# Seven block products for one more group, and the inverse deviation from ScalarE, in a fused attention and MLP kernel

## The chip, the cores and the metric

The kernel runs on one core of a Trainium2 chip. The metric is device time in microseconds (us) of one execution; less is better. Each kernel was run several times beside the kernel before on the same chip. A ratio below is the mean time of one kernel's fast runs over that of the other's fast runs of the same rounds, so it is not quite the ratio of the medians that are quoted beside it. A run counts as slow, and not as fast, when it is over 1.5% above the fastest of the same kernel; the ratios leave these out.

## The reference

Sliding-window attention for 8 batches, 8 heads, 576 positions and 64 channels per head, then a layer norm and a two-layer MLP (512 to 2048 to 512) with a residual:

```python
scores = scale * q @ k.T;  mask = (rel >= 0) & (rel < 64)
attn = softmax(where(mask, scores, -1e9));  x = attn @ v      # (8, 576, 512) after the heads are joined
mu = mean(x);  var = mean((x - mu) ** 2)
xn = (x - mu) / sqrt(var + 1e-06) * g_ln
out = x + relu(xn @ w_ch1) @ w_ch2
```

## The kernel before

The rows are worked in nine groups: groups 0 to 7 are the first 512 positions of each batch, group 8 the last 64 positions of all batches (the "tail", four blocks of 128 rows that are prepared during periods 3, 5 and 7). A *period* is the MLP of one group; the attention of the next group is spread over it in numbered *slots*, one behind each unit of matmuls. The order of every engine's queue is the order in which the program is written.

A block's way through the layer norm: `b_step` (attention times v, normalisation and statistics, on VectorE), `z_step` (the normalised rows `z`, in fp16), `zt_step` (`z` transposed into `zT`, which the first layer multiplies; by a DMA for groups 2 to 7 except the last block of groups 3 and 5, by TensorE for the rest). For groups 2 to 8 `z` is GpSimd's work:

```python
nc.gpsimd.tensor_scalar(out=ve, in0=var, scalar1=1.0, scalar2=EPS, op0=ALU.mult, op1=ALU.add)
nc.gpsimd.tensor_tensor(out=rs, in0=ve, in1=mhalf, op=ALU.pow)
nc.gpsimd.tensor_scalar(out=nm, in0=mu, scalar1=rs, scalar2=-1.0, op0=ALU.mult, op1=ALU.mult)
nc.gpsimd.tensor_scalar(out=z, in0=xv, scalar1=rs, scalar2=nm, op0=ALU.mult, op1=ALU.add)
```

For groups 0 and 1 VectorE only subtracts the mean; the factor (by Newton steps, `newton`) is applied to the output.

The second layer of groups 2 to 8 is done with seven block products instead of eight: 112 matmuls of 256 columns in place of 64 of 512. It needs sums of W2's blocks once (`w2_sums`, eight VectorE operations, two in period 1 and six in period 2) and sums of the hidden activations for every group (`s_sums`, VectorE), and VectorE adds each product to the output (`post`). Groups 0 and 1 use plain products.

```python
# period 1 (g == 1) prepares group 2, slots of b_step, z_step, zt_step
at((13, 17, 20, 23)[j], b_step, 2, j)
at((13, 17, 20, 23)[j], z_step, 2, j)
at((18, 21, 24, 27)[j], zt_step, 2, j)
# ... cut ...
# later periods prepare group b, and the tail's block i
at((2, 7, 12, 17)[j], b_step, b, j);  at((2, 7, 12, 17)[j], z_step, b, j)
ts = (10, 11, 14, 20) if n else (1, 2, 5, 11)
at(ts[2], b_step, NGRP - 1, i);  at(ts[2], z_step, NGRP - 1, i);  at(ts[3], zt_step, NGRP - 1, i)
```

The softmax here doesn't subtract the row's maximum and nothing guards it: scores larger than these inputs give would overflow.

## Time and profile before

| | before |
|---|---|
| median of 4 runs | 314.07 us |
| span of the profiled run | 313.0 us |
| TensorE (PE) busy | 298.9 us, 95% |
| VectorE (DVE), ScalarE (ACT), GpSimd (POOL) busy | 66%, 49%, 53% |
| granted TensorE clock | 0.999 |

The page's first part gives each engine's busy time with its share of the span and its number of instructions:

```profile
PE 298.9 (95%) x3041; PEld 194.1 (62%) x3041; DVE 205.2 (66%) x385; ACT 153.4 (49%) x258; POOL 166.3 (53%) x251
```

The table of windows gives busy time of each engine per stretch; its columns are the stretch, its length, and busy us with the number of instructions for PE, PEld (weight load), DVE, ACT and POOL, then the granted clock, the DMA share and GB/s:

```profile
75.00:98.00 23.00, 22.36 (x240) 11.98 (x238) 14.82 (x38) 9.02 (x15) 12.74 (x23) 1.00 0.62 137
160.00:190.00 30.00, 29.99 (x322) 19.74 (x320) 21.11 (x40) 16.07 (x27) 19.91 (x31) 1.00 1.02 228
```

TensorE has no gap to speak of. Anything that makes it wait is paid in full, and little can be gained elsewhere.

The groups of GpSimd instructions that make `z` (line, engine, operation, output and inputs, count, then busy us and mean ns of one, then idle time ahead of them):

```profile
L345 POOL TENSOR_SCALAR z<-xn,rsz 128x512 f16<-128x512 f32 x28 | 25.3, 902 | 2.9
L343 POOL TENSOR_TENSOR rsz<-rsz,mhalf 128x1 f32<-128x1 f32 x28 | 19.3, 689 | 2.3
L344 POOL TENSOR_SCALAR rsz<-mvg,rsz 128x1 f32<-128x1 f32 x28 | 13.4, 480 | 2.8
L342 POOL TENSOR_SCALAR rsz<-mvg 128x1 f32<-128x1 f32 x28 | 10.7, 382 | 60.4 <-DVE mvg L328 59.8
```

The issue queue of SyncE near the end of period 1, from the timeline (start, us, queue, line, operation):

```profile
93.08 0.33 SPq L430 DMA_DIRECT2D out_dram<-xn  x1
93.50 1.21 SPq L353 DMA_TRANSPOSE zT<-z  x1
```

The last `zT` transpose of group 2 stands behind a store there, and group 2's first matmul starts at 96.43 us: just in time.

### The profile page before, as it was taken

The numbers are of one execution on the slowest core, as the hardware profiler recorded it, in microseconds if no ns is written. First come the engines' busy times: TensorE is split into PE (matmuls) and PEld (weight loads), VectorE is DVE, ScalarE is ACT, GpSimd is POOL, SyncE is SP. The second block draws the span as 40 slices with busy tenths as digits, with TensorE's granted clock in tenths as the row PEclk, the third lists the DMA queues.
The fourth block names the chain that finished last, engine by engine and source line by source line (L and its number), as shares of the span: only waits on it lengthen the run. The fifth ranks groups of instructions, "written<-read, shape, count | busy, mean of one in ns | idle before, by whom it ended". The sixth has DMA issues, their size and how long they took to land.

```text
span 313.0 us, 7473 instructions
## 1 busy us (share of the span) xinstructions
PE 298.9 (95%) x3041; PEld 194.1 (62%) x3041; DVE 205.2 (66%) x385; ACT 153.4 (49%) x258; POOL 166.3 (53%) x251
## 2 busy tenths in 40 slices
PE   6988998899999999999999999999999999999992
PEld 4457544497554468646964686459646855784582
DVE  1689585855674996589666965896669636751642
ACT  1496633477416752776247526762475058306500
POOL 7578666454760798369814983698145506200000
PEclk9999999999999999999999999999999999999999
DMA  8999999998866996798179997993690393003013
GB/s 192 267 390 290 320 336 272 280 304 184 159 144 196 268 206 105 243 312 147 37 212 316 203 149 219 316 142 67 209 172 19 62 209 117 2 2 134 0 36 101
DMA packets 109892, 57.42 MB, mean 183 GB/s; under 512 B 79841, under 2 KB 100833, under 8 KB 109858
## 3 DMA queue, kind: packets, MB, share of 16 engines
q1 hardware_dynamic: 108944, 54.02, 69.1%
q0 software_dynamic: 768, 2.80, 3.7%
q8 instruction: 24, 0.39, 0.5%
q10 hardware_dynamic: 146, 0.13, 0.1%
q14 instruction: 10, 0.08, 0.1%
HBM read 38.80 MB, written 9.44 MB: 154 GB/s over the span
## 4 chain that ended last, share of the span: by engine, by line
PE 74%; DMA 10%; DVE 7%; SPq 4%; POOL 2%; ACT 1%; issue 1%; POOLq 0%; ACTq 0%
PE hps L392 30%; PE pA L464 11%; PE pC L464 7%; PE pB L464 7%; PE ch L404 6%; DMA w2s<-in_moe_w_ch_dram 4%; DMA qk<-in_k_dram 4%; PE xps L317 3%; PE sc L283 3%; PE hph L513 3%; PE tp L226 2%; SPq L141 2%; DVE sS L443 2%; DMA w1s<-in_moe_w_ch_dram 2%; SPq L89 1%; DVE pt L297 1%
## 5 line engine op out<-in xcount | busy, mean ns | idle before, releaser
L392 PE MATMUL hps<-zT,w1g 128*128 128x512 f16 x480 | 110.4, 379 | 0.0
L396 ACT ACTIVATE hrT<-hps 128x512 f16<-128x512 f32 x120 | 71.9, 599 | 50.7 <-PE hps L392 47.2
L392 PEld LDWEIGHTS <-w1g 128*128 128x128 f16 x480 | 44.6, 98 | 49.3 <-issue 1.0
L290 ACT ACTIVATE pt<-sc 128x512 f16<-128x512 f32 x72 | 39.0, 595 | 29.8 <-DVE xn L471 15.6
L464 PEld LDWEIGHTS <-sS 128*128 128x128 f16 x448 | 43.3, 98 | 5.1
L342 POOL TENSOR_SCALAR rsz<-mvg 128x1 f32<-128x1 f32 x28 | 10.7, 382 | 60.4 <-DVE mvg L328 59.8
L128 POOL CAST qk<-qk 128x1024 f16<-128x1024 f32 x32 | 35.1, 1112 | 13.4 <-DMA qk<-in_q_dram 6.9
L464 PEld LDWEIGHTS <-hrT 128*128 128x128 f16 x336 | 32.6, 98 | 5.2
L212 ACT COPY qkT<-tp 128x1024 f16<-128x1024 f16 x16 | 16.1, 1012 | 35.2 <-PE tp L226 26.1
L297 DVE TENSOR_TENSOR pt<-pt,mask 128x1024 f16<-128x1024 f16 x32 | 25.4, 800 | 11.9 <-ACT pt L290 11.9
L471 DVE TENSOR_TENSOR xn<-pA,xn 128x512 f32<-128x512 f32 x28 | 19.2, 686 | 21.1 <-PE pA L464 21.1
L443 DVE TENSOR_TENSOR sS<-hrT 128x512 f16<-128x512 f16 (+1 forms) x42 | 24.8, 591 | 10.2 <-ACT hrT L396 10.2
L464 PE MATMUL pA<-wT,sS 128*128 128x256 f16 x224 | 26.9, 273 | 0.0
L345 POOL TENSOR_SCALAR z<-xn,rsz 128x512 f16<-128x512 f32 x28 | 25.3, 902 | 2.9
L464 PE MATMUL pC<-w2s,sS 128*128 128x256 f16 x224 | 26.8, 273 | 0.0
L325 DVE BATCH_NORM_STATS2 stats<-xn 128x6 f32<-128x512 f32 x36 | 25.0, 695 | 1.2
L323 DVE TENSOR_TENSOR xn<-xps,rcp 128x512 f32<-128x512 f32 x36 | 24.9, 692 | 1.2
L513 PE MATMUL hph<-zT,w1g 128*128 128x256 f16 x192 | 23.2, 272 | 2.3 <-ACT zT L360 1.1
L320 DVE RECIPROCAL rcp<-xps 128x8 f32<-128x8 f32 x36 | 7.4, 205 | 26.8 <-PE xps L317 26.8
L404 PE MATMUL ch<-w2s,hrT 128*128 128x512 f16 x96 | 23.1, 380 | 0.0
L513 PEld LDWEIGHTS <-w1g 128*128 128x128 f16 x192 | 18.3, 98 | 5.1 <-issue 2.6
L317 PEld LDWEIGHTS <-pt 128*64 128x64 f16 x576 | 12.2, 110 | 14.4 <-issue 6.4
(85 smaller groups left out, 395.1 us busy)
## 6 DMA issues: line engine op xcount, KB each, us to landing
out_dram<-xn SPq DMA_DIRECT2D x34, 256.0 KB, 2.6
qk<-in_q_dram SPq DMA_DIRECT2D x16, 512.0 KB, 6.2
qk<-in_k_dram SPq DMA_DIRECT2D x16, 512.0 KB, 7.4
v<-in_v_dram SPq DMA_DIRECT2D x32, 256.0 KB, 6.5
w2s<-in_moe_w_ch_dram SPq DMA_DIRECT2D x12, 512.0 KB, 5.7
w1s<-in_moe_w_ch_dram SPq DMA_DIRECT2D x4, 512.0 KB, 6.7
tk<-in_k_dram SPq DMA_DIRECT2D x8, 256.0 KB, 4.7
tv<-in_v_dram SPq DMA_DIRECT2D x8, 256.0 KB, 5.3
```

Of the source, the lines that this page charges most:

```text
L128: nc.gpsimd.tensor_copy(out=dst[:, :].rearrange("p (a j) e d -> p a e j d", j=j), in_=t[:, :].rearrange("p (a e j d) -> p a e j d", e=2, j ...
L290: nc.scalar.activation(out=o, in_=i, func=AF.Exp, bias=0.0, scale=scale)
L297: nc.vector.tensor_tensor(out=ptv, in0=ptv, in1=mb, op=ALU.mult)
L323: nc.vector.tensor_tensor(out=xn, in0=xps[:, :, 0:D], in1=rcp_b, op=ALU.mult)
L325: nc.vector.bn_stats(out=stats, in_=xv)
L345: nc.gpsimd.tensor_scalar(out=z, in0=xv, scalar1=rs, scalar2=nm, op0=ALU.mult, op1=ALU.add)
L392: nc.tensor.matmul(out=hps, lhsT=w1g[:, kc, 128 * hc:128 * (hc + 1)], rhs=zT[g][:, kc, :], start=(kc == 0), stop=(kc == NKC - 1),)
L396: nc.scalar.activation(out=hrT[:, hc, :], in_=hps, func=AF.Relu, bias=0.0, scale=1.0)
L404: nc.tensor.matmul(out=ch[kb], lhsT=hrT[:, hc, 128 * kb:128 * (kb + 1)], rhs=w2s[:, hc, :], start=(hc == 0), stop=(hc == NHC - 1),)
L443: nc.vector.tensor_tensor(out=o, in0=x, in1=y, op=op)
L464: nc.tensor.matmul(out=bank[which][:, p, :], lhsT=a[:, c, 128 * p:128 * p + 128], rhs=wv[:, c, :], start=(first and p == 0 and c == 0), st ...
L513: nc.tensor.matmul(out=hps[:, e], lhsT=w1g[:, kc, 128 * hc:128 * (hc + 1)], rhs=zT[g][:, kc, 256 * half:256 * half + 256], start=(kc == 0) ...
```

## The change

Intent: save TensorE time by giving group 1 the seven products too, and unload GpSimd by computing the inverse deviation on ScalarE, as exp(-ln(var + eps)/2), with one table set that holds both functions. The core of the diff:

```diff
+    nc.scalar.preload_act_table_set("natural_log_exp_and_others")
 # z_step, groups 1 to 8 (group 0 keeps the subtraction alone)
-        nc.gpsimd.tensor_scalar(out=ve, in0=var, scalar1=1.0, scalar2=EPS, op0=ALU.mult, op1=ALU.add)
-        nc.gpsimd.tensor_tensor(out=rs, in0=ve, in1=mhalf, op=ALU.pow)
-        nc.gpsimd.tensor_scalar(out=nm, in0=mu, scalar1=rs, scalar2=-1.0, op0=ALU.mult, op1=ALU.mult)
-        nc.gpsimd.tensor_scalar(out=z, in0=xv, scalar1=rs, scalar2=nm, op0=ALU.mult, op1=ALU.add)
+        nc.scalar.activation(out=lv, in_=var, func=AF.Ln, bias=epst[:, 0:1], scale=1.0)
+        nc.scalar.activation(out=rs, in_=lv, func=AF.Exp, bias=0.0, scale=-0.5)
+        eng = nc.vector if g == 1 else nc.gpsimd
+        eng.tensor_scalar(out=z, in0=xv, scalar1=mu, scalar2=rs, op0=ALU.subtract, op1=ALU.mult)
 # seven products from group 1 on
-        units, s_sums = mlp_units(g, (8, 16)[g] if g < 2 else 0, g == 0, g > 1)
+        units, s_sums = mlp_units(g, (8, 16)[g] if g < 2 else 0, g == 0, g > 0)
 # W2 sums: from periods 1 and 2 into period 0 (six) and the start of period 1 (two)
+            for m, i in enumerate((3, 2, 4)):
+                at(25 + 2 * m, w2_sums, i, 0, 4)
+                at(26 + 2 * m, w2_sums, i, 4, 8)
 # period 1: k evictions of group 2 on ScalarE, group 1's last zT later
-            at(4, t_main, 2, 1, 0)
+            at(4, t_main, 2, 1, 0, 0)
-            at(6, t_main, 2, 1, 1)
+            at(6, t_main, 2, 1, 1, 0)
-            at(5, zt_step, 1, 3)
+            at(7, zt_step, 1, 3)
 # z three slots after its statistics (two in period 1); zt_step stays
-                at((2, 7, 12, 17)[j], z_step, b, j)
+                at((5, 10, 15, 20)[j], z_step, b, j)
-            at(ts[2], z_step, NGRP - 1, i)
+            at(ts[2] + 3, z_step, NGRP - 1, i)
 ... (other slots of period 1 and buffer orders cut)
```

More of the change, by code (lines that the diff above doesn't have):

```diff
@@ L66 @@
     gT = p_const.tile([128, NKC], FP32, tag="gT", name="gT")
-    mhalf = p_const.tile([128, 1], FP32, tag="mhalf", name="mhalf")
+    epst = p_const.tile([128, 1], FP32, tag="epst", name="epst")
     w1g = p_const.tile([128, NKC, HID], FP16, tag="w1g", name="w1g")
@@ L303, in b_step @@
             if (g, kb // 2) not in x_norm:
-                for h in ((1, 0) if g // 2 == 2 else (0, 1)):
+                for h in ((1, 0) if g in (3, 4, 7) else (0, 1)):
                     x_norm[(g, h)] = p_xn.tile([128, 2, DM], FP32, tag="xn" + sfx, name=f"xn_{g}_{h}", bufs=nb)
@@ L328, in b_step @@
         nc.vector.bn_aggr(out=mvg[g][:, kb, :], in_=stats)
-        if g < 2:
+        if g == 0:
             z_step(g, kb)
@@ L336, in z_step @@
         mu, var = mvg[g][:, kb, 0:1], mvg[g][:, kb, 1:2]
-        if g < 2:
+        if g == 0:
             nc.vector.tensor_scalar(out=z, in0=xv, scalar1=mu, scalar2=None, op0=ALU.subtract)
             return
-        t = p_blk.tile([128, 3], FP32, tag="rsz", name=f"rsz_{g}_{kb}")
-        ve, rs, nm = (t[:, i:i + 1] for i in range(3))
-        nc.gpsimd.tensor_scalar(out=ve, in0=var, scalar1=1.0, scalar2=EPS, op0=ALU.mult, op1=ALU.add)
-        nc.gpsimd.tensor_tensor(out=rs, in0=ve, in1=mhalf, op=ALU.pow)
-        nc.gpsimd.tensor_scalar(out=nm, in0=mu, scalar1=rs, scalar2=-1.0, op0=ALU.mult, op1=ALU.mult)
-        nc.gpsimd.tensor_scalar(out=z, in0=xv, scalar1=rs, scalar2=nm, op0=ALU.mult, op1=ALU.add)
+        t = p_blk.tile([128, 2], FP32, tag="rsz", name=f"rsz_{g}_{kb}")
+        lv, rs = t[:, 0:1], t[:, 1:2]
+        nc.scalar.activation(out=lv, in_=var, func=AF.Ln, bias=epst[:, 0:1], scale=1.0)
+        nc.scalar.activation(out=rs, in_=lv, func=AF.Exp, bias=0.0, scale=-0.5)
+        eng = nc.vector if g == 1 else nc.gpsimd
+        eng.tensor_scalar(out=z, in0=xv, scalar1=mu, scalar2=rs, op0=ALU.subtract, op1=ALU.mult)
     def zt_step(g, kb, eng="act"):
@@ L412, in add_out @@
             xv = x_norm[(g, kb // 2)][:, kb % 2, :]
-            if g < 2:
+            if g == 0:
                 nc.vector.scalar_tensor_tensor(
@@ L576 @@
     nc.vector.memset(ones1, 1.0)
-    nc.vector.memset(mhalf, -0.5)
+    nc.vector.memset(epst, EPS)
     nc.gpsimd.affine_select(
@@ L689 @@
             at(18, b_step, 1, 0)
+            at(20, z_step, 1, 0)
             at(21, b_step, 1, 1)
-            at(22, zt_step, 1, 0)
-            at(24, zt_step, 1, 1)
+            at(23, z_step, 1, 1)
+            at(23, zt_step, 1, 0)
+            at(26, zt_step, 1, 1)
+            for m, i in enumerate((3, 2, 4)):
+                at(25 + 2 * m, w2_sums, i, 0, 4)
+                at(26 + 2 * m, w2_sums, i, 4, 8)
             at(26, t_main, 1, 0, 1, 0)
@@ L705 @@
             at(0, cast_qk, 2, 0)
-            at(0, cast_qk, 2, 1)
+            at(2, cast_qk, 2, 1)
             at(1, b_step, 1, 3)
-            at(2, zt_step, 1, 2)
-            at(13, newton, 1, 0, 4)
-            at(5, zt_step, 1, 3)
+            at(1, z_step, 1, 2)
+            at(4, z_step, 1, 3)
+            at(2, w2_sums, 1, 0, 4)
+            at(3, w2_sums, 1, 4, 8)
+            at(3, zt_step, 1, 2)
+            at(7, zt_step, 1, 3)
+            for i in range(1, 5):
+                at((12, 12, 13, 14)[i - 1], s_sums, 0, 4, i)
+                at((16, 16, 18, 20)[i - 1], s_sums, 4, 8, i)
             at(4, alloc_v, 2)
@@ L716 @@
             at(4, t_main, 2, 0, 0)
-            at(4, t_main, 2, 1, 0)
+            at(4, t_main, 2, 1, 0, 0)
             at(6, t_main, 2, 0, 1)
-            at(6, t_main, 2, 1, 1)
-            at(25, w2_sums, 3, 0, 4)
-            at(28, w2_sums, 3, 4, 8)
+            at(6, t_main, 2, 1, 1, 0)
             for j in range(4):
@@ L725 @@
                 at((13, 17, 20, 23)[j], b_step, 2, j)
-                at((13, 17, 20, 23)[j], z_step, 2, j)
+                at((15, 19, 22, 25)[j], z_step, 2, j)
                 at((18, 21, 24, 27)[j], zt_step, 2, j)
@@ L738 @@
             at(17, make_vB, 3)
-            at(31, s_mm, 3, 0)
-            at(31, s_mask, 3, 0)
-            for i, (x, half) in zip((12, 24, 12, 28), ((0, 0), (1, 0), (0, 1), (1, 1))):
+            at(28, s_mm, 3, 0)
+            at(29, s_mask, 3, 0)
+            for i, (x, half) in zip((12, 22, 12, 25), ((0, 0), (1, 0), (0, 1), (1, 1))):
                 at(i, t_main, 3, x, half, 0)
@@ L745 @@
             at(40, load_v, 4, 0, 4)
-        if g == 2:
-            for m, i in enumerate((2, 1, 4)):
-                at(4 + 2 * m, w2_sums, i, 0, 4)
-                at(5 + 2 * m, w2_sums, i, 4, 8)
         if g > 1 and g + 2 < B:
@@ L807 @@
         for i, u in enumerate(units):
-            if g > 1 and i == 20:
+            if g > 0 and i == 20:
                 tbank["shared"] = True
```

## The prediction

> **What bounds it now.** TensorE. The page has PE busy 298.9 of 313.0 us at granted clock 0.999. The table of windows puts PE at 30.00 of 30 us in each stretch from 160 to 280 us; the idle lies at the start (about 3 us), in the load-bound time up to 47.75 us (the last wait there, 1.06 us, is for the W2 cast) and in the tail. So only a shorter matmul stream, or a wait removed between 48 and 129 us, pays.
>
> **What the change does, costed from the trace.**
> - Group 1's second layer: 64 matmuls of 512 columns (16 take 3.46 us in the chain, 13.8 us in all) become 112 of 256 columns (16 take 1.75 us, 12.2 us in all): -1.6 us, all on the critical path.
> - Group 1's Newton steps go: the PE wait on rstmp (0.64 us at 76.5) goes.
> - W2 sums leave period 2 (8 x 0.68 us of VectorE, which is 95% busy from 100 to 120 us) for periods 0 and 1. Period 2 lasts 32.1 us against 31.5 for the next ones: about -0.7 us there. In period 0 the six sums fit VectorE's gaps.
> - GpSimd loses 28 x (382+689+480) ns = 43 us of small operations: off the critical path. Each z now waits for Ln and Exp on one column. The Trainium skill, "ScalarE: Activation LUTs", section "What ACT_TABLE_LOAD costs", gives 186 ns fixed and 93 ns per pointer operand; the trace's 599 ns for 512 columns agrees with its 186+0.833N. My estimate from it: 0.47 us per block, some 15 us of ScalarE in all, mostly hidden: z comes three slots after its statistics. One table load (1.28 us) stays.
>
> **What it costs.**
> - First half of period 1 (from 58.75 us): ScalarE gets two more transpose evictions (1.01 us each, formerly VectorE's), two Ln/Exp pairs, and the last zT copy comes directly before the unit that needs it. By hand from the durations, with z(1,2) also later, the ninth unit starts 1.5 to 2.4 us later than before (69.85 us). I take +1.9.
> - End of period 1: the fourth zT transfer of group 2 stands in the DMA issue queue behind two stores that wait for the fourth product's addition, two units before the period's end. Before, addition-to-landing took: addition end 93.05, transpose issued 93.50, landing about 3 us later, and PE needed it at 96.43: just in time. Now the additions end about 1.3 us after that product, two issues of 0.35 us, 3 us landing: about 5 us, against about 2.1 us of remaining PE work. New PE stall about 2.8 us.
>
> **Sum.** -1.6 -0.6 -0.7 +1.9 +2.8 = +1.8; shaded a little towards the author's intent: predicted 315.4 us, 80% range 312.3 to 317.8. Chances: faster by over 2% 0.02, within 2% 0.95, slower by over 2% 0.03.
>
> **What would show each step.** Group 1's product matmuls at L464 16 per 1.75 us; one ACT_TABLE_LOAD; GpSimd busy near 125 us; PE idle of 2 to 3 us at about 97 us, before group 2's first hps, with the transpose of z issued after two stores; zT or eviction waits of about 2 us between 62 and 72 us, ScalarE near full there; periods from group 3 on unchanged at 31.5 us.
>
> **What would make it wrong.** If the zT transfer lands earlier than I count, or ScalarE keeps up in period 1, the result is 311 to 312 us. If Ln/Exp take much longer than 0.47 us, or the in-order ScalarE waits for statistics and holds up the Relu evictions (hps has two buffers, and the Relu loop of 0.21+0.60+0.05 us just equals a unit's 0.865 us), every period loses some tenths: 318 or more.

## The result, and the profile after

The change made the kernel slower: 331.45 us median of 4 runs (329.91 to 332.74) against 314.07, ratio of the fast runs 1.0529 with a 95% interval from 1.0463 to 1.0595. The prediction, 315.4 with a range up to 317.8, was wrong.

The page's first part, now of the changed kernel:

```profile
PE 302.6 (91%) x3089; PEld 199.6 (60%) x3089; DVE 213.8 (65%) x383; ACT 167.9 (51%) x324; POOL 166.3 (50%) x167
```

And the groups that make `z` in it (source lines are shifted by one):

```profile
L346 POOL TENSOR_SCALAR z<-xn,mvg,rsz 128x512 f16<-128x512 f32 x28 | 66.8, 2388 | 81.8 <-ACT rsz L344 62.2 <-DMA tv<-in_v_dram 8.8 <-DVE sS L444 8.4
...
L343 ACT ACTIVATE rsz<-mvg,epst 128x1 f32<-128x1 f32 x32 | 9.2, 289 | 25.9 <-DVE mvg L329 25.9
...
L344 ACT ACTIVATE rsz<-rsz 128x1 f32<-128x1 f32 x32 | 6.5, 203 | 1.0
```

GpSimd lost 84 small instructions and is exactly as busy as before: 19.3 + 13.4 + 10.7 = 43.4 us of small operations went, and `z` itself rose from 25.3 to 66.8 us. The same 128x512 operation takes 2388 ns in place of 902. Ln and Exp cost what was estimated: 289 ns for one column with a bias pointer and 203 ns without. The Trainium skill, "ScalarE: Activation LUTs", section "What ACT_TABLE_LOAD costs", was right here: its formula gives 280 and 187 ns. One table load of 1283 ns in all served Exp, Ln, Relu and copies.

What TensorE waited for (who, for whom, us in total, times, longest; the line of `warm` is the start and was 2.9 us before too):

```profile
PE ztp L358 <- POOL z L346: 5.4, 5, 1.7
PE xps L318 <- DVE pt L298: 3.4, 3, 2.5
PE hps L393 <- DMA zT<-z: 2.9, 2, 2.3
PE warm L594 <- DVE mbias L587: 2.9, 1, 2.9
PE hph L514 <- ACT zT L361: 2.7, 3, 1.5
```

Where the time went can be read by phases. I took from TensorE's timeline the start of each group's first-layer matmuls (L1) and second-layer matmuls (L2); the table gives us from one start to the next, for the profiled runs. L2 of a period ends where the next group's L1 begins.

| phase | before | after | r2 | r4 | r5 | r8 | r12 |
|---|---|---|---|---|---|---|---|
| period 0 L2 | 20.5 | 23.4 | 22.6 | 20.1 | 20.3 | 22.3 | 20.2 |
| period 1 L1 | 20.2 | 24.2 | 21.9 | 19.0 | 19.9 | 23.3 | 21.1 |
| period 1 L2 | 17.5 | 19.6 | 20.2 | 17.5 | 17.6 | 18.2 | 18.2 |
| period 2 L1 | 16.3 | 16.3 | 18.0 | 16.3 | 16.3 | 16.3 | 16.4 |
| period 2 L2 | 15.8 | 16.5 | 15.1 | 15.8 | 15.8 | 15.1 | 15.0 |
| period 3 L1 | 17.5 | 18.8 | 19.3 | 19.3 | 17.8 | 19.3 | 17.5 |
| period 3 L2 | 14.1 | 14.1 | 14.1 | 14.1 | 14.8 | 14.1 | 14.1 |
| period 4 L2 | 15.0 | 17.7 | 15.1 | 15.1 | 15.1 | 15.3 | 15.1 |
| period 5 L1 | 17.5 | 18.8 | 19.3 | 19.3 | 17.8 | 19.3 | 17.5 |
| period 5 L2 | 14.1 | 14.1 | 14.1 | 14.1 | 14.8 | 14.1 | 14.1 |
| period 6 L2 | 12.7 | 13.5 | 12.7 | 12.7 | 12.7 | 12.7 | 12.7 |
| period 7 L1 | 16.8 | 18.5 | 16.9 | 16.9 | 16.9 | 16.9 | 16.8 |

The phases that are left out differ by little (the first layer of period 0 by up to 1.3 us, in the load-bound start). After minus before, the listed phases add to +17.8 us; the spans differ by 18.0. So the loss has two halves: +9.7 us from period 0's second layer to period 2, and +8.1 us in periods 3 to 7, which the prediction had called unchanged. Single profiles vary: r2 and r8 hold the same program up to slot 26 of period 1, and yet differ by 0.3 us in period 0's second layer and by 1.4 us in period 1's first.

Three details of the first half. In period 0, five of the six W2 sums take 1.09 to 1.52 us, where all eight took 0.66 to 0.69 us before, and the mask of the scores stands behind them. First one such sum before, then VectorE's timeline in the changed kernel, then TensorE's, with the wait in brackets:

```profile
92.97 0.68 DVE L561 TENSOR_TENSOR wT<-w2s 128x1024 f16<-128x1024 f16 x1
```

```profile
49.61 2.52 DVE L562 TENSOR_TENSOR wT<-w2s 128x1024 f16<-128x1024 f16 x2
...
54.86 1.52 DVE L562 TENSOR_TENSOR wT<-wT,w2s 128x1024 f16<-128x1024 f16 x1
...
56.87 1.41 DVE L562 TENSOR_TENSOR wT<-w2s,wT 128x1024 f16<-128x1024 f16 x1
58.20 1.52 DVE L298 TENSOR_TENSOR pt<-pt,mask 128x1024 f16<-128x1024 f16 x1
```

```profile
59.77 0.22 PE L318 MATMUL xps<-vB,pt 128*64 128x65 f16 x1 [2.50 <-DVE pt L298]
```

At the end of period 1 the transpose of the last `z` is issued behind two stores (SyncE's queue), and TensorE waits for it:

```profile
101.87 0.83 SPq L431 DMA_DIRECT2D out_dram<-xn  x2
102.79 1.21 SPq L354 DMA_TRANSPOSE zT<-z  x1
```

```profile
105.64 2.75 PE L393 MATMUL hps<-zT,w1g 128*128 128x512 f16 x12 [2.33 <-DMA zT<-z]
```

And the windows show a granted clock below 1 in period 1, which the kernel before does not have (its windows first, then those of the changed kernel):

```profile
60.00:70.00 10.00, 9.03 (x114) 8.16 (x114) 6.44 (x12) 6.82 (x11) 4.67 (x9) 1.00 0.92 268
70.00:80.00 10.00, 9.36 (x124) 7.30 (x122) 5.99 (x19) 7.23 (x13) 5.05 (x6) 1.00 0.91 198
```

```profile
60.00:70.00 10.00, 8.73 (x90) 6.07 (x85) 6.67 (x14) 3.81 (x8) 3.67 (x5) 0.83 0.89 248
70.00:80.00 10.00, 8.13 (x88) 6.47 (x86) 0.74 (x1) 7.80 (x15) 4.96 (x6) 0.86 1.13 214
```

Before the last 2 us of its span, the clock records of that run hold two intervals of 3.41 us at half clock, from 60.11 and from 77.18 us. The Trainium skill, "TensorE: Matmul & The Clock Gate", section "What's actually happening", says that the activity window is 3413 ns and free-running, and names two states of the clock, full and half; the 3.41 us and the 0.5 of these records agree.

### The profile page after: what moved, and what is told of

The parts are those of the page before. It is cut to its first block, busy times and chain, and to the rows that moved or that the text cites. A ratio compares the mean times of both kernels' runs of the same rounds, so it can differ in the third digit from the quotient of the medians.

```text
span 331.0 us, 7566 instructions
## 1 busy us (share of the span) xinstructions
PE 302.6 (91%) x3089; PEld 199.6 (60%) x3089; DVE 213.8 (65%) x383; ACT 167.9 (51%) x324; POOL 166.3 (50%) x167
## 4 chain that ended last, share of the span: by engine, by line
PE 49%; DMA 14%; SPq 11%; DVE 9%; POOL 8%; issue 4%; ACT 3%; POOLq 0%; ACTq 0%; DVEq 0%
PE hps L393 20%; PE pA L465 9%; DMA qk<-in_k_dram 6%; POOL z L346 6%; PE pB L465 6%; PE pC L465 5%; SPq L142 4%; PE hph L514 4%; DMA zT<-z 3%; DMA w2s<-in_moe_w_ch_dram 2%; PE xps L318 2%; PE sc L284 2%; DVE wT L562 2%; DMA w1s<-in_moe_w_ch_dram 1%; DVE sS L444 1%
## 5 line engine op out<-in xcount | busy, mean ns | idle before, releaser
L346 POOL TENSOR_SCALAR z<-xn,mvg,rsz 128x512 f16<-128x512 f32 x28 | 66.8, 2388 | 81.8 <-ACT rsz L344 62.2
L465 PEld LDWEIGHTS <-sS 128*128 128x128 f16 x512 | 49.2, 98 | 6.4 <-issue 0.2
L291 ACT ACTIVATE pt<-sc 128x512 f16<-128x512 f32 x72 | 39.0, 594 | 26.9 <-PE sc L284 25.2
L465 PEld LDWEIGHTS <-hrT 128*128 128x128 f16 x384 | 37.1, 98 | 5.8
L444 DVE TENSOR_TENSOR sS<-hrT 128x512 f16<-128x512 f16 (+1 forms) x46 | 30.3, 658 | 11.4 <-ACT hrT L397 10.2
L472 DVE TENSOR_TENSOR xn<-pA,xn 128x512 f32<-128x512 f32 x32 | 21.9, 685 | 23.0 <-PE pA L465 22.8
L298 DVE TENSOR_TENSOR pt<-pt,mask 128x1024 f16<-128x1024 f16 x32 | 23.4, 738 | 17.6 <-ACT pt L291 17.6
L465 PE MATMUL pA<-wT,sS 128*128 128x256 f16 x256 | 30.9, 273 | 0.2
L465 PE MATMUL pC<-w2s,sS 128*128 128x256 f16 x256 | 30.9, 273 | 0.0
L514 PE MATMUL hph<-zT,w1g 128*128 128x256 f16 x192 | 25.3, 288 | 3.3 <-ACT zT L361 2.7
L343 ACT ACTIVATE rsz<-mvg,epst 128x1 f32<-128x1 f32 x32 | 9.2, 289 | 25.9 <-DVE mvg L329 25.9
L519 ACT ACTIVATE hrT<-hph 128x512 f16<-128x512 f32 x24 | 14.3, 601 | 15.3 <-PE hph L514 15.1
```

The source lines that it names most:

```text
L291: nc.scalar.activation(out=o, in_=i, func=AF.Exp, bias=0.0, scale=scale)
L298: nc.vector.tensor_tensor(out=ptv, in0=ptv, in1=mb, op=ALU.mult)
L346: eng.tensor_scalar(out=z, in0=xv, scalar1=mu, scalar2=rs, op0=ALU.subtract, op1=ALU.mult)
L444: nc.vector.tensor_tensor(out=o, in0=x, in1=y, op=op)
L465: nc.tensor.matmul(out=bank[which][:, p, :], lhsT=a[:, c, 128 * p:128 * p + 128], rhs=wv[:, c, :], start=(first and p == 0 and c == 0), st ...
L472: nc.vector.tensor_tensor(out=xv, in0=bank[which], in1=xv, op=ALU.add)
```

## The experiments

### r1: the operation by itself

The kernel before, with ten forms of a 128x512 operation (fp32 in, fp16 out) appended on GpSimd behind all other work, each form ten times on a line of its own:

```diff
+    for _ in range(10):
+        gp.tensor_scalar(out=my, in0=mx, scalar1=p, scalar2=r, op0=ALU.mult, op1=ALU.add)           # L825
+        gp.tensor_scalar(out=my, in0=mx, scalar1=p, scalar2=r, op0=ALU.subtract, op1=ALU.mult)      # L826
+        gp.tensor_scalar(out=my, in0=mx, scalar1=o, scalar2=r, op0=ALU.subtract, op1=ALU.mult)      # L827: o from another tile
+        gp.tensor_scalar(out=my, in0=mx, scalar1=o, scalar2=r, op0=ALU.mult, op1=ALU.add)           # L828: o from another tile
+        gp.tensor_scalar(out=my, in0=mx, scalar1=p, scalar2=r, op0=ALU.add, op1=ALU.mult)           # L829
+        gp.tensor_scalar(out=my, in0=mx, scalar1=p, scalar2=r, op0=ALU.mult, op1=ALU.subtract)      # L830
+        gp.tensor_scalar(out=my, in0=mx, scalar1=p, scalar2=r, op0=ALU.mult, op1=ALU.mult)          # L831
+        gp.tensor_scalar(out=my, in0=mx, scalar1=0.5, scalar2=0.5, op0=ALU.subtract, op1=ALU.mult)  # L832
+        gp.tensor_scalar(out=my, in0=mx, scalar1=p, scalar2=None, op0=ALU.subtract)                 # L833
+        gp.tensor_scalar(out=my, in0=mx, scalar1=p, scalar2=r, op0=ALU.subtract, op1=ALU.add)       # L834
```

> The kernel before, with ten forms of a one-input operation on a 128x512 fp32 tile with fp16 output appended on GpSimd, repeated ten times after all other work. In the changed kernel z as (x - mu) * rs took 2.07 us at least, in the kernel before z as x * rs + nm took 0.76 us at least. Theory F (the pair of operations decides): every form with subtract then mult takes 2.0 us or more, also with both scalars from one tile and with immediates, and mult then add takes 0.76 us also with scalars from two tiles. Rival P (the place of the scalars decides: mu comes from the statistics tile, rs from another): both pairs take 0.76 us with scalars of one tile and 2 us with scalars of two tiles. Rival C (contention of that kernel's schedule): all forms take about 0.76 us in the quiet end. The total time only grows by the appended work.

The groups of GpSimd instructions in the quiet end, from 320 us on:

```profile
L834 POOL TENSOR_SCALAR my<-mx,mp 128x512 f16<-128x512 f32 x8 | 16.6, 2077 | 0.8
L830 POOL TENSOR_SCALAR my<-mx,mp 128x512 f16<-128x512 f32 x7 | 14.6, 2083 | 0.7
L826 POOL TENSOR_SCALAR my<-mx,mp 128x512 f16<-128x512 f32 x7 | 14.5, 2077 | 0.7
L827 POOL TENSOR_SCALAR my<-mx,mo,mp 128x512 f16<-128x512 f32 x7 | 14.5, 2073 | 0.7
L832 POOL TENSOR_SCALAR my<-mx 128x512 f16<-128x512 f32 x7 | 13.5, 1932 | 0.6
L833 POOL TENSOR_SCALAR my<-mx,mp 128x512 f16<-128x512 f32 x7 | 10.9, 1562 | 0.7
L828 POOL TENSOR_SCALAR my<-mx,mo,mp 128x512 f16<-128x512 f32 x7 | 5.4, 768 | 0.7
L825 POOL TENSOR_SCALAR my<-mx,mp 128x512 f16<-128x512 f32 x7 | 5.4, 767 | 0.7
L829 POOL TENSOR_SCALAR my<-mx,mp 128x512 f16<-128x512 f32 x7 | 5.4, 767 | 0.7
L831 POOL TENSOR_SCALAR my<-mx,mp 128x512 f16<-128x512 f32 x7 | 5.4, 767 | 0.7
```

Every pair of add and mult that was tried takes 767 ns, whatever the order and wherever the scalars come from. Every pair with a subtract takes about 2.08 us (1.93 with immediates), in either place; a lone subtract takes 1.56. It was not expected that the place of the subtract makes no difference. The total, 436.6 us, is only the appended work. Theory F holds in the wider form "subtract is slow"; the rivals fall. The Trainium skill, "GPSIMD Engine Reference", section "3.1 Elementwise — side-by-side cycle accounting", gives 769 ns as measured for 512 elements in the best case; the 767 ns here agree, but the page says nothing of a subtract.

### r2: the changed kernel with z in its old form

```diff
-        eng.tensor_scalar(out=z, in0=xv, scalar1=mu, scalar2=rs, op0=ALU.subtract, op1=ALU.mult)
+        nc.gpsimd.tensor_scalar(out=nm, in0=mu, scalar1=rs, scalar2=-1.0, op0=ALU.mult, op1=ALU.mult)
+        nc.gpsimd.tensor_scalar(out=z, in0=xv, scalar1=rs, scalar2=nm, op0=ALU.mult, op1=ALU.add)   # groups 2 to 8
```

> The changed kernel with z on GpSimd for groups 2 to 8 written as before, x * rs + nm, with nm = -mu * rs from one more 128x1 GpSimd operation (0.3 to 0.5 us); everything else as changed. Theory F: z falls from 2.4 to 0.8 us, the stretches from group 2's second layer on return to the lengths of before (they lost 8.8 us together), and some of period 1's loss: 319 to 323 us. Rival (the wait on ScalarE's Ln and Exp and the later z slots are what costs): 328 to 332 us, as the changed kernel.

Measured: 325.49 us, ratio 1.0368 (1.0326 to 1.0410), against 1.0529 for the whole change. `z` took 912 ns, and the second layers of periods 4 and 6 and the first of period 7 came back (17.7 to 15.1, 13.5 to 12.7, 18.5 to 16.9 us). But the total missed the expected range from above, and the first layers of periods 3 and 5 stayed long (19.3 us). The form is a part, about 1.6% of the time in this schedule, not the whole.

### r3: the kernel before with the new form of z

```diff
-        nc.gpsimd.tensor_scalar(out=nm, in0=mu, scalar1=rs, scalar2=-1.0, op0=ALU.mult, op1=ALU.mult)
-        nc.gpsimd.tensor_scalar(out=z, in0=xv, scalar1=rs, scalar2=nm, op0=ALU.mult, op1=ALU.add)
+        nc.gpsimd.tensor_scalar(out=z, in0=xv, scalar1=mu, scalar2=rs, op0=ALU.subtract, op1=ALU.mult)
```

> The kernel before with only the form of z changed: (x - mu) * rs on GpSimd in place of nm and x * rs + nm; pow, slots and the rest as before. Theory F: z takes 2.1 to 2.7 us, net 1.1 us more per block on the way to the transposes, in slots three earlier than in the changed kernel: 315 to 322 us, slower than before in the second layers of groups 4 and 6 and first layers of 3, 5, 7. Rival (form is free): 313 to 314 us.

Measured: 323.34 us, ratio 1.0321 (1.0281 to 1.0361), a little above the expected range. `z` took 2306 ns. One rewritten expression, which even drops an instruction, costs 3.2% by itself. TensorE's waits of this run show how: GpSimd's queue runs late, so besides `z` its casts of q and k come late. Of the phases that were expected to grow, the second layer of period 4 (15.0 to 17.2 us) and the first of period 7 (16.8 to 17.7) did; the first layers of periods 3 and 5 and the second of period 6 did not, and the second layers of periods 1, 2, 3 and 5 grew instead, by 2.1, 1.8, 1.1 and 1.1 us.

```profile
PE tp L226 <- POOL qk L128: 3.5, 7, 0.9
PE ztp L356 <- POOL z L344: 2.4, 3, 0.9
```

### r4 and r5: Ln and Exp, and the later slots

r4 is the kernel before with Ln and Exp in place of add and pow for groups 2 to 8, the preloaded table set and the later slots of `z`, in its old form. r5 is r4 with one number changed:

```diff
-            at(ts[2] + 3, z_step, NGRP - 1, i)
+            at(ts[2] + 1, z_step, NGRP - 1, i)
```

> The kernel before with Ln and Exp on ScalarE in place of add and pow on GpSimd for groups 2 to 8, the preloaded joint table, and the z slots three later as in the change; z in its old form x * rs + nm. Theory F: Ln and Exp by themselves cost nothing, since ScalarE has room and z takes about 0.8 us: 313 to 316 us. Rival (Ln and Exp in ScalarE's in-order queue hold up the Relu evictions): 318 us or more, with every period some tenths longer.

> r4_lnexp with one number changed: the z of the tail blocks (group 8) one slot after its statistics step, not three. Theory S (the later slot puts this z into VectorE's burst of block sums, where it took 2.17 us instead of 0.76, and its transposes made TensorE wait 1.64 us in period 3): the first layers of periods 3 and 5 return from 19.3 to 17.4 us each, and the total from 317.9 to 313.5 to 315 us. Rival (Ln and Exp ahead of the Relus cost the time whatever the slot): within 1 us of r4_lnexp, 317 to 319 us.

r4 measured 317.92 us, ratio 1.0137 (1.0103 to 1.0171), more than expected for a harmless change, and less than the rival said; not every period grew, but the first layers of 3 and 5 (17.5 to 19.3 us each). r5 measured 316.51 us, ratio 1.0071 (1.0035 to 1.0106). The two first layers went to 17.8 us, as the slot theory says, and neither the rival nor the full return came true: the second layers of periods 3 and 5 grew by 0.7 us, where TensorE waits for VectorE's additions (0.54 us at 150.86 us). r5 stays 0.7% slower than before, nearly all of it in these four phases.

Why the slot matters is to be read in r4 at 139 us, first in GpSimd's timeline, then VectorE's, then TensorE's:

```profile
134.98 0.76 POOL L346 TENSOR_SCALAR z<-xn,rsz 128x512 f16<-128x512 f32 x1
138.52 0.78 POOL L345 TENSOR_SCALAR rsz<-mvg,rsz 128x1 f32<-128x1 f32 x1 [2.77 <-ACT rsz L344]
139.40 2.17 POOL L346 TENSOR_SCALAR z<-xn,rsz 128x512 f16<-128x512 f32 x1
```

```profile
138.48 0.69 DVE L444 TENSOR_TENSOR sS<-hrT 128x1024 f16<-128x1024 f16 x1
139.20 0.69 DVE L444 TENSOR_TENSOR sS<-sS,hrT 128x1024 f16<-128x1024 f16 x1
139.81 0.68 DVE L444 TENSOR_TENSOR sS<-hrT 128x1024 f16<-128x1024 f16 x1
140.41 0.68 DVE L444 TENSOR_TENSOR sS<-hrT,sS 128x1024 f16<-128x1024 f16 x1
```

```profile
141.63 0.40 PE L358 MATMUL ztp<-ident,z 128*128 128x128 f16 x4 [1.64 <-POOL z L346]
```

The same `z` instruction that takes 0.76 us takes 2.17 while VectorE's four two-input sums run, and ends just after them. Before, this `z` came ahead of the burst. The Trainium skill, "GPSIMD Engine Reference", section "1. Specifications", says that GpSimd shares its SBUF interfaces with VectorE and names two SBUF inputs as a case of contention; this agrees in kind, and the page gives no size. That these sums are the cause of this one delay is shown by r5 only as far as moving `z` out of their way removes the 1.64 us wait; no run made the sums go away alone.

So Ln and Exp gave nothing: the 30 us of pow and add that left GpSimd in r4 were not on TensorE's path, and their place in the queue mattered more than their length.

### r6: the W2 sums out of period 0

```diff
-            for m, i in enumerate((3, 2, 4)):
-                at(25 + 2 * m, w2_sums, i, 0, 4);  at(26 + 2 * m, w2_sums, i, 4, 8)      # period 0
-            at(2, w2_sums, 1, 0, 4);  at(3, w2_sums, 1, 4, 8)                           # period 1
+            for m, i in enumerate((3, 2, 4, 1)):
+                at(8 + m, w2_sums, i, 0, 4);  at(8 + m, w2_sums, i, 4, 8)               # period 1
```

> r2_multadd with all eight W2 sums moved out of period 0 and the start of period 1 into slots 8 to 11 of period 1, where VectorE idled 9 us in the changed kernel. Theory W (in period 0 the sums hold up the mask of the scores, and TensorE waits 1.9 us or more for it): the second layer of period 0 returns from 22.6 to about 20.5 us, so 322 to 324 us against 325.5. Rival (that time is lost to the load of W2 or q and k, not to the sums): period 0 keeps 22 us or more and the total stays at 325 to 326.

Measured: 325.58 us, ratio 1.0368 (1.0338 to 1.0399): no change in total against r2. But both halves of the answer are in the phases: period 0's second layer fell from 22.6 to 20.9 us, as theory W says (r7 and r8, whose period 0 is that of r2, took 21.7 and 22.3), and period 1's second layer rose from 20.2 to 21.7, with a new wait of 1.36 us for the mask there. The work was moved, and so was the wait.

### r7: the evictions of period 1

```diff
-            at(4, t_main, 2, 1, 0, 0);  at(6, t_main, 2, 1, 1, 0)     # evicted by ScalarE
+            at(4, t_main, 2, 1, 0);     at(6, t_main, 2, 1, 1)        # by VectorE, as before
-            at(4, z_step, 1, 3);  at(7, zt_step, 1, 3)
+            at(3, z_step, 1, 3);  at(5, zt_step, 1, 3)
```

> r2_multadd with the two k transposes of group 2 evicted by VectorE as before, and the last z and zT of group 1 one and two slots earlier. Theory E (ScalarE's queue, with four evictions of 1 us, holds up the last zT copy, and TensorE waits 0.35 + 1.51 us): the first layer of period 1 falls from 21.9 to 19 to 20.5 us, and the total to 322.5 to 324.5 us. Rival (the start of the period, waiting for the mask and the additions, is what costs): period 1's first layer stays above 21 us.

Measured: 323.96 us, ratio 1.0317 (1.0286 to 1.0348). Period 1's first layer fell from 21.9 to 20.4 us and the wait for the `zT` copies from 2.7 to 1.1 us. Theory E holds for that layer; the edit changes two things at once, so their shares stay open. Part of the gain went again: period 1's second layer rose from 20.2 to 21.0 us. Period 0's second layer, which the edit does not touch, was 1.0 us shorter in this profile, so the total (ratio lower by 0.0051, about 1.6 us) says less than the phase.

### r8: the transpose ahead of the stores

```diff
-                at((18, 21, 24, 27)[j], zt_step, 2, j)
+                at((18, 21, 24, 26)[j], zt_step, 2, j)
```

> r2_multadd with the transpose of group 2's last z issued one slot earlier, before the two stores in the same issue queue, not after them. Theory Z (the prediction's step: the stores wait for an addition and hold up the transpose): TensorE's wait of 2.33 us for zT before group 2's first hps falls below 1 us, the half-clock interval after it goes, and the total falls by 2 to 4 us to 321.5 to 323.5. Rival (z itself is late): the wait stays above 1.5 us and the total within 1 us of 325.5.

Measured: 322.40 us, ratio 1.0274 (1.0246 to 1.0301). The wait of 2.33 us for `zT` is gone, and so is the half-clock interval that followed it in r2. SyncE's queue in r2 and then in r8:

```profile
99.01 0.83 SPq L434 DMA_DIRECT2D out_dram<-xn  x2
99.94 1.21 SPq L357 DMA_TRANSPOSE zT<-z  x1
```

```profile
88.05 12.29 SPq L357 DMA_TRANSPOSE zT<-z  x4
100.44 0.53 SPq L434 DMA_DIRECT2D out_dram<-xn  x1
```

The windows with the start of period 2, first of r2 (102.78 us), then of r8 (about 101.8 us):

```profile
103.00:107.00 4.00, 4.00 (x12) 1.35 (x10) 0.00 (x0) 1.19 (x2) 0.00 (x0) 0.60 0.99 306
```

```profile
103.00:107.00 4.00, 4.00 (x49) 1.96 (x47) 2.04 (x6) 3.24 (x6) 0.00 (x0) 1.00 0.89 256
```

In r2 the wait is followed by 3.41 us at half clock from 102.77 us on (0.60 in this window): period 2's first layer took 18.0 us against 16.3. In r2, one issue slot thus cost a wait of 2.33 us and about 1.7 us of slower matmuls. In the changed kernel the same wait of 2.33 us was not followed by half clock, and period 2's first layer took 16.3 us. The saving in the total is less than their sum (ratio lower by 0.0094, about 3 us), because period 1's first layer was longer in r8's profiled run (23.3 us), with a wait of 1.88 us for group 1's third `z` that r2 has with 0.43; why it varies is open.

### r9 to r12: can the seven products be made to pay?

r9 joins the mends (old form of `z`, tail slot, evictions, transposes, W2 sums in slots 4 to 8 of period 1, masks of group 2 earlier). r10 is r9 with groups 2 to 8 wholly as before, so that only the seven products for group 1 remain of the change:

```diff
+        if g == 1:          # Ln and Exp only here; z on VectorE
+        ...                 # else: add, pow, nm, x * rs + nm on GpSimd, at the old slots
```

> The change with every fault found so far mended: z on GpSimd as x * rs + nm, the tail's z one slot after its statistics, k evictions of group 2 on VectorE, the last zT of group 1 earlier, group 2's last transpose ahead of the stores, W2 sums in slots 4 to 8 of period 1 and the masks of group 2 one or two slots earlier. If the separate effects add (from 325.5: -1.8 -1.8 for the tails, -1.5 evictions, -3.1 transpose, -1.8 sums in period 0, masks -1 to -1.5): 314 to 316 us. If there is a further cost not found yet: 318 or more.

> As r9, but for groups 2 to 8 z is wholly as before (add, pow, nm, x * rs + nm on GpSimd, at the old slots); Ln and Exp only for group 1, whose z is VectorE's. What remains of the change is seven products for group 1. If the gain of the prediction is real (-1.6 us of matmuls, -0.6 Newton wait, -0.7 in period 2) and Ln and Exp give nothing for groups 2 to 8: 310.5 to 312.5 us, below both kernels. If seven products bring no gain even when well placed: 313 to 315.

r9: 319.06 us, ratio 1.0140 (1.0101 to 1.0179), above its range; its runs scatter and its profile is not read further. The separate effects did not add up, and the further cost of which its expectation warned is not located. r10: 315.41 us, ratio 1.0058 (1.0030 to 1.0087). It differs from r9 only in how and in which slots `z` of groups 2 to 8 is made, so Ln, Exp and their slots cost even the mended kernel about 0.8% (1.0140 against 1.0058). Still r10 is no faster than before, though all phases from period 2 on are within 0.2 us of before or shorter (period 2's second layer 15.0 against 15.8 us). In its profiled run (317.16 us, the slowest of its six) the loss is in period 1, where VectorE was busy 35.6 us between 58 and 98 us, against 25.2 before.

r11 relieves VectorE there (k evictions on ScalarE again, two sums in period 0, the others in slots 5 to 8), and r12 also swaps an order:

```diff
-            at((13, 17, 20, 23)[j], b_step, 2, j);  at((13, 17, 20, 23)[j], z_step, 2, j)
+            at((13, 17, 21, 23)[j], b_step, 2, j);  at((13, 17, 21, 23)[j], z_step, 2, j)
```

> r10 with VectorE relieved in period 1, where it was busy 35.6 of 40 us against 25.2 before: the k evictions of group 2 on ScalarE (2.4 us less for VectorE), the first two W2 sums in period 0's gap, the other six in slots 5 to 8. If VectorE's load is what turned the gain of the seven products into waits (sc for qkT 1.7 us, pA for an addition 1.1 us and the half-clock interval after it): period 1 falls from 41.5 to 37 us or less and the total to 311 to 313 us, below the kernel before. If it is something else: 314.5 us or more.

> r11 with group 2's third attention block one slot later in period 1, so that VectorE does the addition of product 6 before that block's four operations, not after them. If that order caused pA's wait of 1.1 us in r11: the wait goes, and the total falls by about 1 us to 313 to 314 us, level with the kernel before or just below. If VectorE is simply full from 75 to 97 us, the wait only moves: 314.5 to 315.5 us.

r11: 314.95 us, ratio 1.0024 (1.0000 to 1.0048). r12: 314.90 us, ratio 1.0033 (0.9999 to 1.0068). Both are level with the kernel before at best; r11's expected 311 to 313 us did not come. In r12 the wait of pA for the addition went, and a wait of 1.27 us of the next block for VectorE came in its place: the wait only moved. A second wait, of 1.31 us, is for the last `zT` transfer of group 2; r11 waits 0.81 us there, for VectorE's addition:

```profile
89.67 0.22 PE L319 MATMUL xps<-vB,pt 128*64 128x65 f16 x1 [1.27 <-DVE xn L325]
97.67 0.59 PE L399 MATMUL hps<-zT,w1g 128*128 128x512 f16 x2 [1.31 <-DMA zT<-z]
```

The window of period 1's second layer in r12, to be held against that of before (same stretch, shown above; the kernels are within 1.3 us of each other there):

```profile
75.00:98.00 23.00, 20.42 (x280) 16.84 (x275) 20.30 (x36) 8.68 (x15) 14.06 (x23) 1.00 0.53 111
```

TensorE has fewer columns to do here, but it is idle for 2.58 us (23.00 - 20.42) where it was idle for 0.64; VectorE has 5.48 us more to do, 20.30 of 23 us; and the phase is no shorter (18.2 us against 17.5). The two waits are that idle time. That the transfer was late because VectorE's statistics were late is not shown; no run issues it earlier from r12. No version beat the kernel before, so none is offered.

## Why the prediction was wrong

The sum forecast +1.8 us; the medians differ by 17.4. Step by step, in the prediction's terms:

- *Gain on TensorE, -1.6 us.* The work did shrink (112 matmuls, 16 per 1.75 us), but it never became time. The step left out its price on VectorE: the additions and sums of activations that seven products bring into period 1. In every version whose profile was read, TensorE then waits for VectorE there (in r12 for 1.27 us, and 1.31 us more for a transfer), and r12 shows 5.5 us more VectorE work in 23 us.
- *Newton wait, -0.6, and period 2, -0.7 us.* Right: the wait on Newton steps is gone, and period 2's second layer fell from 15.8 to about 15.0 us once `z` had its old form (r2, r8, r12). Only six of the eight W2 sums had been in period 2, not all eight.
- *"GpSimd loses 28 x (382+689+480) ns = 43 us".* This is the step that failed first. The sum is right to 0.4 us, but the prediction never costed the operation that was rewritten and kept: it took `z` at its old duration ("GpSimd busy near 125 us"; it was 166.3). With a subtract it takes 2.08 us instead of 0.77 (r1), and GpSimd's busy time did not fall at all. Alone that costs 3.2% in the old schedule (r3) and 1.6% of the 5.3% in the new one (whole change against r2).
- *"Mostly hidden: z comes three slots after its statistics".* Wrong in sign. The later slots put the tail's `z` into VectorE's burst of sums, where even the fast form takes 2.17 us, with the transposes left at their old slots: +1.8 us in each of the first layers of periods 3 and 5 (r4; r5 undoes 1.5 us of each).
- *"In period 0 the six sums fit VectorE's gaps".* Wrong. They were costed at 0.68 us; five of them took 1.09 to 1.52 us, while GpSimd was casting q, k and v; the mask came late, TensorE waited 2.50 us, and half clock followed. Period 0's second layer grew by 2.9 us, and by 2.1 in r2; r6, without sums there, has 0.4 left. No run isolates the casts, but the traces side with them: in all profiled runs but r9, 31 of the 44 W2 sums that ran beside a GpSimd cast took 1.08 to 2.50 us, and of the 60 that did not, 59 took 0.66 to 0.69 and one, beside a `z` with a subtract (r3), 1.07.
- *First half of period 1, +1.9.* The mechanism was right, and the size too where it can be read (+1.7 us in r2, 1.5 of it undone by r7). But r8, with the same program there, has +3.1, and the changed kernel +4.0, with two half-clock intervals in or next to it; how much these cost is not shown.
- *zT behind two stores, +2.8.* Right: TensorE waited 2.33 us, and r8 removes it with one slot. Not foreseen: a half-clock interval after it in r2 (not in the changed kernel), another 1.7 us.
- *"Periods from group 3 on unchanged".* Wrong, +8.1 us, by the form of `z` and the slots together.

The named risks ("Ln/Exp take much longer", "ScalarE holds up the Relus") were the wrong ones: Ln and Exp took 0.49 us together against the 0.47 estimated. The largest single cost that a run isolated was in the one instruction whose output and size had not changed; the rest is several smaller waits, which did not add up when they were mended together (r9).

## What to carry to other kernels

Where a change rewrites an expression algebraically, cost the new form of the operation on its engine, not only the operations that come and go; a short list of forms appended at the quiet end of a kernel answers it in one run. When TensorE is full, moving work between the other engines is decided by order and by what runs beside it, not by busy time: look at which burst the moved instruction will meet, and keep a latency-critical DMA ahead of stores in the same issue queue. And a saving on the bound engine that adds three times as much work to an engine with little room in that stretch can come back as waits, as here (1.6 us forecast as saved, 5.5 us added, VectorE then busy 20.3 of 23 us).

## What the Trainium skill lacked or had wrong

- "GPSIMD Engine Reference", section 3.1: no cost by kind of operation. A 128x512 two-step scalar operation with add and mult took 767 ns, with a subtract in either step 2.07 to 2.08 us (1.93 with immediates), and a lone subtract 1.56 us (r1).
- "GPSIMD Engine Reference", section 1: the contention with VectorE is named there without a size; the skill has more on it elsewhere, but no figures for these pairs. The same GpSimd operation took 0.76 us alone and 2.17 us beside VectorE's two-input sums (r4). VectorE's W2 sums took 0.66 to 0.69 us in the kernel before, and five of them 1.09 to 1.52 us in period 0 of the changed kernel, while GpSimd was casting; no run isolates this second pair.
- "TensorE: Matmul & The Clock Gate", section "Why this matters for your kernels", advises against idle gaps over about 3 us. Here shorter ones were followed by 3.41 us at half clock: 2.50 and 1.51 us (changed kernel) and 2.33 us (r2). Others were not: 2.33 us at 105.64 us (changed kernel), 1.94 us (r2) and 1.88 us (r8). So the length of a gap does not decide alone. In the clock records of all these runs the clock changes only at whole multiples of 3.413 us from its first change to full. Counted in these windows, half clock followed each one with TensorE busy for under 1.1 us (0.91 us from 56.70 us in the changed kernel, 1.09 us from 99.36 us in r2) and none with 1.72 us or more; in between, from 1.49 to 1.67 us, it followed some. The 2.33 us that half clock did not follow were cut by the edge of a window at 104.48 us, with 2.23 and 2.25 us busy on its two sides.
